# Attention scores from float32 tiles or from three float16 products of cast and added halves

## Chip, core and metric

The kernel runs on one core of a Trainium2 chip. The metric is device time in microseconds of one execution, median of several runs. TensorE (PE) multiplies, VectorE (DVE) and ScalarE (ACT) work on elements, GpSimd (POOL) does some of both, and SP (SyncE) issues transfers. Each engine works through its own instructions in order and waits at an instruction until what it needs is there.

## What is computed

Inputs are q, k, v of 8 batches, 8 heads, 576 positions and 64 values per head. Attention is local: each head's sequence is cut into 9 chunks of 64, and each chunk attends to itself alone.

```python
scores = scale * np.matmul(q_c, k_c.transpose(0, 1, 2, 4, 3))
scores = scores - np.max(scores, axis=-1, keepdims=True)
attn = np.exp(scores)
attn = attn / (np.sum(attn, axis=-1, keepdims=True) + 1e-09)
out = np.matmul(attn, v_c)
```

The result x (8 x 576 x 512) goes through two feed-forward layers: `x + relu(norm(x) @ w_ch1) @ w_ch2`, and then a gated layer with a product over positions and `w_out`. Everything is float32 outside; the kernel writes most products as three float16 products of a high and a low half (high·high, high·low, low·high).

## The kernel before

Attention runs in 36 units t = 0 to 35, each of 128 rows (two chunks side by side) and 8 heads; two units make a block b = t // 2 of the first feed-forward layer. The input `qkv` holds q, k and v of a unit as 128 rows of 1536 float32, q and k next to each other with the head dimension along the partitions.

The order of all work is written by a planner, `Plan`. Each `op(engine, ns, fn, rd, wr, prio, lat)` is an operation with its cost, what it reads and writes, and the latency until other engines see its result. The planner plays a clock: of the operations that are ready on an engine it places the one with the lowest `prio`. The engine then executes in that order, whatever real durations are.

From block 3 on, blocks and attention are merged. For each block, eight steps `ff1p` (L750, first product into two PSUM banks in turn, 24 matmuls, later read by ScalarE at L765) and `ff2p` (L802, second product, two steps behind). Between them L772 to L774 form sums on VectorE, L777 on ScalarE makes the high half and L778 on VectorE the low half. After the steps of block b, the attention units of block b + 2 are emitted (`block(b + 2)`), and the planner mixes them in. The tile names `arena`, `acc` and `bank` belong to this part.

One unit t >= 10 (`JOIN`) goes through these operations:

- `scores(t)`: SP loads q and k (512 KB) into `qkl`, one buffer (L283). `qk` multiplies 16 pairs of 64x64 float32 tiles into `pair` (L291), in four quadrants of the array; the profile shows two records for each float32 multiplication.
- `attention(t)`: maximum (L389), subtraction into `pml` (L390), exponential on ScalarE (L393); `vl` is loaded on SP (L319).
- From t = 14 (`BYDMA`) on, `pml` is split into float16 halves `ph` (L400 on ScalarE, L401 on VectorE), SP transposes them by a transfer into `ptt` (L404), v is split into `vq` (L408, L409), and `pv_` makes 48 float16 products (L349). Units t = 10 to 13 transpose on TensorE into a float32 tile `pt` and multiply in float32 (L361).
- `pv_` of t and `qk` of t + 1 are one planned operation on TensorE (L429): it waits for `ptt`, `vq` and the q and k of the next unit.
- `norm(t)`: statistics (L462, L463), `rs` on GpSimd (L457, L460), `xn` (L466), halves `hl` (L469 on ScalarE, L471 on GpSimd, two buffers), and a transposing transfer on SP into `xT` (L267), which has two buffers and so waits until the first products of block b - 2 are through.

At a block's end L825 and L830 read the sums out of PSUM, L835 on GpSimd adds them, and SP stores them to `x2d` (L677).

Of the kernel before, what the change touches and what calls it, by code (L numbers as in the profile page):

```python
# [9 lines left out]
F16 = mybir.dt.float16  # L10
F32 = mybir.dt.float32
# [3 lines left out]
AF = mybir.ActivationFunctionType  # L15
ALU = mybir.AluOpType
# [8 lines left out]
    a=[2264, -1991, -1698, -26, -1734, 4025, 2562, -374],  # L25
# [4 lines left out]
    lo=[1, 0, 0, 0, 0, 1, 1, 1],  # L30
# [8 lines left out]
    xn=[0, 1, 0, 0, 1, 1, 1, 1],  # L39
    g=[150, 12000, 200, 400, 150],  # L40
    f=[-277, -1680, 2543],
# [9 lines left out]
JOIN = 10  # L51
# [96 lines left out]
def fused_kernel(ctx: ExitStack, tc, qkv, w1, w2, g1, w_in, w_out, wsgt, wsgs, g2, b_sg, out):  # L148
    nc = tc.nc
    PSUM = bass.MemoryType.PSUM  # L150
    P = 128
# [20 lines left out]
    pools = {}  # L172
# [42 lines left out]
    plan = Plan(TUNE['g'][1])  # L215
# [55 lines left out]
    def palloc(tag, bufs, shape, dt, pool=None):  # L271
        return plan.buf(tag, bufs, lambda: (pool or pools["att"][1]).tile(shape, dt, tag=tag, name=tag, bufs=bufs))
# [3 lines left out]
    started = {}  # L276
    BYDMA = 14

    def scores(t, o):

        a = palloc("qk", 2, [P, 2, 512], F32) if t < JOIN else palloc("qkl", 1, [P, 2, 512], F32)
        src = qkv[t].rearrange("p (a f) -> p a f", a=3)
        o("SP", 1700, lambda: nc.sync.dma_start(out=a.t, in_=src[:, 0:2]), wr=[a], lat=2200 if t < JOIN else 4000)  # L283
        s2 = pair[t % 2 if t < 6 else 1]

        def qk():
            for hp in range(4):
                for r in (slice(0, 64), slice(64, 128)):
                    for c in range(2):
                        k = hp * 128 + c * 64  # L290
                        nc.tensor.matmul(  # L291
                            s2[64 * c:64 * c + 64, r.start // 64, hp * 64:hp * 64 + 64],
                            lhsT=a.t[r, 0, k:k + 64],
                            rhs=a.t[r, 1, k:k + 64],
                            start=True,
                            stop=True,
                        )

        started[t] = a, qk

    def attention(t):
        n = t % 2 if t < 6 else 1
        s2, ks = pair[n], f"pair{n}"
        kp = ks if t < JOIN else "pairv"
        pr = TUNE['a'][t] if t < 8 else 10 * t
        lat = TUNE['g'][2] if t < 8 else 300 if t < JOIN else 600 if t < JOIN + 2 else 1000 if t < BYDMA else 400
        far = dict(lat=1500 if t < JOIN + 2 else 3000 if t < BYDMA else 1000) if t >= JOIN else {}
        z = 1

        def o(eng, ns, fn, **k):  # L310
            ns = FAST.get((eng, ns), ns)
            op(eng, ns, fn, prio=k.pop("prio", pr), lat=k.pop("lat", lat), **k)

        if t not in started:
            scores(t, o)
            a, qk = started[t]
            o("PE", 1260 * z, qk, rd=[a], wr=[ks])
        v = palloc("v", 2, [P, 512], F32) if t < JOIN else palloc("vl", 1, [P, 512], F32)
        o("SP", 730, lambda: nc.sync.dma_start(out=v.t, in_=qkv[t].rearrange("p (a f) -> p a f", a=3)[:, 2]), wr=[v], lat=2200)  # L319
        mx = palloc("mx", 2, [P, 2, 4, 1], F32)  # L320
        pm = palloc("pm", 2, [P, 4, 2, 64], F32) if t < JOIN else palloc("pml", 1, [P, 4, 2, 64], F32)
        sm = palloc("sm", 2, [P, 4, 2, 1], F32)
        rd = palloc("rd", 2, [P, 4, 2, 1], F32)
        pt = palloc("pt", 1, [P, 4, 128], F32) if t < BYDMA else None
        if t in (4, 5):
            x = plan.buf(f"x{t}", 1, lambda: pools["att"][1].tile([P, 512], F32, name=f"x{t}", bufs=1))
        else:
            x = palloc("x", 6, [P, 512], F32, px)
# [3 lines left out]
        ptt, vq = [None], [None]  # L332
        pp = lambda: [pt, v] if t < BYDMA else [ptt[0], vq[0]]
# [7 lines left out]
        def pv_():  # L341
            if t >= BYDMA:
                for hp in range(4):
                    for n, (y, z) in enumerate(((0, 0), (0, 1), (1, 0))):
                        for r in (slice(0, 64), slice(64, 128)):
                            for c in range(2):
                                k = c * 256 + hp * 64
                                q = hp * 128 + c * 64
                                nc.tensor.matmul(  # L349
                                    s2[64 * c:64 * c + 64, r.start // 64, 256 + hp * 64:256 + hp * 64 + 64],  # L350
                                    lhsT=ptt[0].t[r, y, q:q + 64],
                                    rhs=vq[0].t[r, z, k:k + 64],
                                    start=(n == 0),
                                    stop=(n == 2),
                                )
                return
            for hp in range(4):
                for r in (slice(0, 64), slice(64, 128)):
                    for c in range(2):
                        k = c * 256 + hp * 64  # L360
                        nc.tensor.matmul(  # L361
                            s2[64 * c:64 * c + 64, r.start // 64, 256 + hp * 64:256 + hp * 64 + 64],
                            lhsT=pt.t[r, hp, 64 * c:64 * c + 64],
                            rhs=v.t[r, k:k + 64],
                            start=True,
                            stop=True,
                        )
# [12 lines left out]
        def sums():  # L380
# [10 lines left out]
            out=pm.t.rearrange("p h a k -> p a h k"), in0=sv, in1=mx.t.to_broadcast([P, 2, 4, 64]), op=ALU.subtract  # L391
# [4 lines left out]
        else:  # L396
            ph = palloc("ph", 1, [P, 2, 512], F16)
# [4 lines left out]
                out=ph.t[:, 1], in0=flat(), in1=ph.t[:, 0], op=ALU.subtract  # L402
            ), rd=[pm], wr=[ph], two=1)
            o("SP", 1100, lambda: nc.sync.dma_start_transpose(  # L404
                out=ptt[0].t.rearrange("p x (h q) -> p (x h) q", h=4), in_=ph.t.rearrange("p x f -> p (x f)")
# [4 lines left out]
                out=vq[0].t[:, 1], in0=v.t, in1=vq[0].t[:, 0], op=ALU.subtract  # L410
# [4 lines left out]
        if t < BYDMA:  # L415
            o("ACT", 480, lambda: nc.scalar.activation(
                out=pt.t.rearrange("p (a h) q -> p a h q", a=2),
                in_=s2[:, :, 0:256].rearrange("p a (h q) -> p a h q", h=2),
                func=AF.Copy,
# [4 lines left out]
        if t < JOIN or t + 1 == NT:  # L424
            o("PE", 1260 * z, pv_, rd=pp(), wr=[kp])
        else:
            scores(t + 1, o)
            a_, qk_ = started[t + 1]
            o("PE", 1260, lambda: (pv_(), qk_()), rd=pp() + [a_], wr=[kp, ks])  # L429
        o("DVE", 600, lambda: nc.vector.tensor_tensor(  # L430
            out=x.t.rearrange("p (h a d) -> p a h d", h=4, a=2),
            in0=pv,
# [6 lines left out]
    def norm(t, x, o):  # L439

        bs = palloc("bs", 2, [P, 6], F32)
        mv = palloc("mv", 2, [P, 2], F32)
        rs = palloc("rs", 2, [P, 1], F32)
        xn = palloc("xn", 1, [P, 512], F32)
        hl = palloc("hl", 2, [P, 2, 512], F16)
        b = t // 2
        c0 = (t % 2 if b < B0 else 1 - t % 2) * 128
        if t % 2 == 0:
            if b == 2:
                xT_t[b] = plan.buf("xT2", 1, lambda: stage.tile([P, 2, 4, 256], F16, name="xT2"))  # L450
            else:
                xT_t[b] = palloc("xT", 2, [P, 2, 4, 256], F16, px)
        xT = xT_t[b]
        x_t[t] = x

        def rs_():
            nc.gpsimd.tensor_scalar(  # L457
                out=rs.t, in0=mv.t[:, 1:2], scalar1=1.0, scalar2=1e-6, op0=ALU.mult, op1=ALU.add
            )
            nc.gpsimd.tensor_tensor(out=rs.t, in0=rs.t, in1=cpow, op=ALU.pow)  # L460

        o("DVE", 600, lambda: nc.vector.bn_stats(out=bs.t, in_=x.t), rd=[x], wr=[bs])  # L462
        o("DVE", 70, lambda: nc.vector.bn_aggr(out=mv.t, in_=bs.t), rd=[bs], wr=[mv])  # L463
        o("POOL", 730, rs_, rd=[mv, "cpow"], wr=[rs], two=2)
        xe = ("POOL", 830, nc.gpsimd) if t < 8 and TUNE['xn'][t] else ("DVE", 460, nc.vector)
        o(xe[0], xe[1], lambda: xe[2].tensor_scalar(  # L466
            out=xn.t, in0=x.t, scalar1=mv.t[:, 0:1], scalar2=rs.t, op0=ALU.subtract, op1=ALU.mult
        ), rd=[x, mv, rs], wr=[xn], two=1 + (xe[0] == "POOL"))
        o("ACT", 520, lambda: nc.scalar.activation(out=hl.t[:, 0], in_=xn.t, func=AF.Copy), rd=[xn], wr=[hl])  # L469
        lo = ("DVE", 600, nc.vector) if t < 8 and TUNE['lo'][t] else ("POOL", 1110, nc.gpsimd)  # L470
        o(lo[0], lo[1], lambda: lo[2].tensor_tensor(  # L471
            out=hl.t[:, 1], in0=xn.t, in1=hl.t[:, 0], op=ALU.subtract
        ), rd=[xn], wr=[hl], two=1)
        o("SP", 1100, lambda: transpose(xT.t, slice(c0, c0 + 128), hl.t), rd=[hl], wr=[xT], lat=2200)
# [379 lines left out]

    bW = {"top": Buf("topB", None)}

    ATT = [f"{n}{k}" for n in ("qk", "v", "mx", "pm", "sm", "rd", "bs", "mv", "rs", "hl") for k in range(2)] + ["pt", "xn", "qkl", "vl", "u0", "u1", "pml", "ph", "ptt", "vq"]
    w2s = {}

    def open_sums():  # L860
# [232 lines left out]
    with tc.manual_schedule():  # L1093
# [127 lines left out]
        vl = fixed("vl", 1, [P, GT, D], F16)  # L1221
# [461 lines left out]
```

## Time and profile before

| | us |
|---|---|
| median of three runs | 1177.54 |
| lowest and highest | 1176.41 and 1178.52 |
| the profiled execution, its own time | 1177.76 |
| its span, first to last instruction | 1175.7 |
| TensorE busy | 1163.7 |
| VectorE busy | 915.2 |
| ScalarE busy | 586.3 |
| GpSimd busy | 196.5 |

The profile's times count from the first instruction of the span. A matmul record is listed with its start and a modelled length, so small matmuls overlap in the list; the distance between starts is the pace. A timeline row merges neighbours: length is from the first start to the last end, and x48 is the number of records. "Landing" of a transfer is the time from issue to its data being there.

### The profile page before, as it was taken

How to read it: one execution, taken by the hardware profiler on the slowest of the kernel's cores; microseconds unless marked ns; L12 is line 12 of the kernel's file. 1: busy time of each engine (PE TensorE's matmuls, PEld its weight loads, DVE VectorE, ACT ScalarE, POOL GpSimd, SP SyncE). 2: the span in 40 equal slices, each digit the busy share in tenths (PEclk: the TensorE clock that was granted, in tenths of full speed). 3: DMA queues.
4: the chain of work that ended last, by engine and by line, in shares of the span. 5: the costliest groups of instructions: out<-in, count | busy, mean ns of one | idle time of the engine just before them, and what ended most of it. 6: DMA issues, size and time to landing. Idle time of an engine off the chain costs nothing.

```text
span 1175.7 us, 27945 instructions
## 1 busy us (share of the span) xinstructions
PE 1163.7 (99%) x11810; PEld 884.4 (75%) x11810; DVE 915.2 (78%) x1744; ACT 586.3 (50%) x854; POOL 196.5 (17%) x279
## 2 busy tenths in 40 slices
PE   8899999999999999999999999999999999999998
PEld 6687448888888888888888888888565566557454
DVE  6997797898898888768877865677889589577555
ACT  5787634665665644434444443345646445434330
POOL 2211010323113112211311322012102001102100
PEclk7999999999999999999999999999999999999999
DMA  8974016544242343244133111436175573372303
GB/s 286 281 242 118 18 28 225 185 111 91 75 93 69 68 100 91 65 82 91 55 89 75 56 46 33 88 86 179 38 140 158 113 149 110 91 123 73 90 1 117
DMA packets 165053, 124.36 MB, mean 106 GB/s; under 512 B 128704, under 2 KB 137792, under 8 KB 164928
## 3 DMA queue, kind: packets, MB, share of 16 engines
q1 hardware_dynamic: 164928, 122.58, 40.2%
q8 instruction: 92, 1.51, 0.5%
q14 instruction: 33, 0.27, 0.1%
HBM read 72.74 MB, written 18.88 MB: 78 GB/s over the span
## 4 chain that ended last, share of the span: by engine, by line
PE 92%; DVE 4%; DMA 2%; ACT 1%; issue 1%; POOL 0%; SPq 0%; ACTq 0%; DVEq 0%
PE bank L750 26%; PE acc L802 23%; PE pb L1478 5%; PE acc L1562 4%; PE pair L659 4%; PE pb L1562 4%; PE acc L1478 3%; PE pb L1382 3%; PE bank L638 3%; PE acc L1424 3%; PE pb L1424 3%; PE acc L1382 3%; PE bank L659 2%; PE pair L291 1%; PE pair L349 1%; PE pb L1479 1%
## 5 line engine op out<-in xcount | busy, mean ns | idle before, releaser
L750 PE MATMUL bank<-xT,w1h 128*128 128x256 f16 x1920 | 321.0, 273 | 0.0
L802 PEld LDWEIGHTS <-arena 128*128 128x128 f16 x2520 | 244.5, 98 | 29.7 <-DVE arena L778 0.2
L750 PE MATMUL bank<-xT,w1l 128*128 128x256 f16 x960 | 261.7, 273 | 0.0
L802 PE MATMUL acc<-w,arena 128*128 128x256 f16 x1440 | 218.3, 273 | 0.0
L750 PEld LDWEIGHTS <-w1h 128*128 128x128 f16 x1920 | 187.7, 98 | 22.1
L777 ACT ACTIVATE arena<-arena 128x896 f16<-128x896 f32 x120 | 113.9, 949 | 159.3 <-DVE arena L774 75.4
L802 PE MATMUL acc<-w2s,arena 128*128 128x256 f16 x1080 | 177.2, 273 | 0.0
L778 DVE TENSOR_TENSOR arena<-arena 128x896 f16<-128x896 f32 x120 | 130.3, 1086 | 39.5 <-ACT arena L777 39.1
L765 ACT ACTIVATE arena<-bank 128x512 f32<-128x512 f32 x120 | 71.4, 595 | 121.2 <-PE bank L750 120.6
L835 POOL TENSOR_TENSOR x<-x,u 128x256 f32<-128x256 f32 (+1 forms) x65 | 62.6, 989 | 259.2 <-DVE x L825 157.7
L750 PEld LDWEIGHTS <-w1l 128*128 128x128 f16 x960 | 93.9, 98 | 10.8
L772 DVE TENSOR_TENSOR arena<-arena 128x256 f32<-128x256 f32 x120 | 57.2, 477 | 37.1 <-ACT arena L765 36.1
L1562 PEld LDWEIGHTS <-w2s 128*128 128x128 f16 x444 | 43.4, 98 | 47.3
L1382 PEld LDWEIGHTS <-x2T 128*128 128x128 f16 x672 | 65.6, 98 | 9.8
L638 PE MATMUL bank<-xT,w1h 128*128 128x256 f16 x384 | 64.4, 273 | 1.1 <-DMA xT<-hl 0.7
L773 DVE TENSOR_TENSOR arena<-arena 128x256 f32<-128x256 f32 x120 | 59.1, 492 | 4.1
L1424 PEld LDWEIGHTS <-late 128*128 128x128 f16 x336 | 32.7, 98 | 39.2
L471 POOL TENSOR_TENSOR hl<-xn,hl 128x512 f16<-128x512 f32 x32 | 43.1, 1346 | 72.9 <-ACT hl L469 68.6
L1478 PEld LDWEIGHTS <-vh 128*128 128x128 f16 x288 | 28.6, 99 | 33.2
L1562 PE MATMUL acc<-wout,w2s 128*128 128x512 f16 (+1 forms) x252 | 53.3, 369 | 0.0
L638 PE MATMUL bank<-xT,w1l 128*128 128x256 f16 x192 | 52.3, 273 | 0.0
L1478 PE MATMUL pb<-wsg,vh 128*128 128x512 f16 x166 | 51.6, 380 | 0.0
(287 smaller groups left out, 2050.7 us busy)
## 6 DMA issues: line engine op xcount, KB each, us to landing
straw<-in_w SPq DMA_DIRECT2D x16, 1023.8 KB, 6.2
qkl<-in_qkv SPq DMA_DIRECT2D x26, 512.0 KB, 3.9
x2d<-x SPq DMA_DIRECT2D x36, 256.0 KB, 2.0
xs<-x2d SPq DMA_DIRECT2D x27, 256.0 KB, 4.2
vl<-in_qkv SPq DMA_DIRECT2D x26, 256.0 KB, 3.2
w2s<-x2d SPq DMA_DIRECT2D x21, 256.0 KB, 2.8
out<-w2s SPq DMA_DIRECT2D x21, 256.0 KB, 3.1
qk<-in_qkv SPq DMA_DIRECT2D x10, 512.0 KB, 4.8
```

The costliest lines, as they stand in the source:

```text
L638: nc.tensor.matmul(acc, lhsT=w[j][:, k, fc], rhs=xT.t[:, x, k], start=(n == 0), stop=(n == 11))
L659: nc.tensor.matmul(acc[i], lhsT=h[x].t[:, c], rhs=w2t[j][:, f % 2, y], start=(f == 0 and n == 0), stop=(f == NF - 1 and n == 2),)
L750: nc.tensor.matmul(acc[:, y * 256:y * 256 + 256], lhsT=w[j][:, k, fc], rhs=xT.t[:, x, k], start=(n == 0), stop=(n == 11),)
L765: op("ACT", 500, lambda: nc.scalar.activation(out=o.t[:, 0:4].rearrange("p n t -> p (n t)"), in_=acc, func=AF.Relu, scale=0.5), rd=[kb] + ...
L777: op("ACT", 860, lambda: nc.scalar.activation(out=h.t[:, 0], in_=o.t[:, 1:8], func=AF.Copy), rd=[o] + ar, wr=[h], prio=-100)
L778: op("DVE", 1010, lambda: nc.vector.tensor_tensor(out=h.t[:, 1], in0=o.t[:, 1:8], in1=h.t[:, 0], op=ALU.subtract), rd=[o, h], wr=[h.key + ...
L802: nc.tensor.matmul(acc, lhsT=h.t[:, x, n], rhs=r(y), start=(first and j == 0 and m == 0), stop=(j == 7 and m == 2), skip_group_check=True,)
L835: op("POOL", ns, lambda: nc.gpsimd.tensor_tensor(out=d(), in0=d(), in1=v(), op=ALU.add), rd=u + ["q6", "q5", "q7"], wr=[x], prio=-50, two=1)
L1382: nc.tensor.matmul(ap[:, q * 256:q * 256 + 256], lhsT=xT[:, x, a, k, c], rhs=right(b, 1, k, w), start=(first and n == 0), stop=(k == 1 and ...
L1424: nc.tensor.matmul(ap, lhsT=right(b, 0, k, w)[:, m * 128:m * 128 + 128], rhs=xT[:, x, a, k], start=(first and n == 0), stop=(k == 1 and w ...
L1478: nc.tensor.matmul(ap, lhsT=v[:, fc], rhs=w[:, 0:512], start=(n == 0), stop=end)
L1562: nc.tensor.matmul(ap[:, 0:m], lhsT=x[:, k, c], rhs=w[:, k, fc], start=(n == 0), stop=(n == 11))
```

## The change

From t = 10 on, q and k are no longer loaded as float32. A transfer issued by GpSimd casts them to float16 on the way into `qh`; ScalarE writes the negative of `qh` into `ql`; a second transfer from GpSimd reads q and k again and adds them to `ql`, which then holds the low half. `qh` and `ql` have two buffers each. The scores are three float16 products (48 matmuls in place of 16 float32 ones). The latencies handed to the planner are 7000, 3000 and 8000 ns. To make room, `hl` has one buffer from t = 10 on (`hll`), and `pt` of t = 10 to 13 lies in the buffer of `ptt`. The product of the two low halves is left out, as in the kernel's other split products.

```diff
     def scores(t, o):
-        a = palloc("qk", 2, [P, 2, 512], F32) if t < JOIN else palloc("qkl", 1, [P, 2, 512], F32)
         src = qkv[t].rearrange("p (a f) -> p a f", a=3)
-        o("SP", 1700, lambda: nc.sync.dma_start(out=a.t, in_=src[:, 0:2]), wr=[a], lat=2200 if t < JOIN else 4000)
         s2 = pair[t % 2 if t < 6 else 1]
+        if t >= JOIN:
+            hi, lo = (palloc(n, 2, [P, 2, 512], F16) for n in ("qh", "ql"))
+            o("POOL", 700, lambda: nc.gpsimd.dma_start(out=hi.t, in_=src[:, 0:2]), wr=[hi], lat=7000)
+            o("ACT", 1050, lambda: nc.scalar.activation(out=lo.t, in_=hi.t, func=AF.Copy, scale=-1.0), rd=[hi], wr=[lo], lat=3000)
+            o("POOL", 920, lambda: nc.gpsimd.dma_start(
+                out=lo.t, in_=src[:, 0:2], accum_op=ALU.add
+            ), wr=[lo], lat=8000)
+
+            def qk():
+                for hp in range(4):
+                    for n, (y, z) in enumerate(((hi, hi), (hi, lo), (lo, hi))):
+                        for r in (slice(0, 64), slice(64, 128)):
+                            for c in range(2):
+                                k = hp * 128 + c * 64
+                                nc.tensor.matmul(
+                                    s2[64 * c:64 * c + 64, r.start // 64, hp * 64:hp * 64 + 64],
+                                    lhsT=y.t[r, 0, k:k + 64],
+                                    rhs=z.t[r, 1, k:k + 64],
+                                    start=(n == 0),
+                                    stop=(n == 2),
+                                )
+
+            started[t] = [hi, lo], qk
+            return
+        a = palloc("qk", 2, [P, 2, 512], F32)
+        o("SP", 1700, lambda: nc.sync.dma_start(out=a.t, in_=src[:, 0:2]), wr=[a], lat=2200)
...
-        pt = palloc("pt", 1, [P, 4, 128], F32) if t < BYDMA else None
+        pt = None
+        if t < JOIN:
+            pt = palloc("pt", 1, [P, 4, 128], F32)
+        elif t < BYDMA:
+            pt = plan.buf("ptt", 1, lambda: pools["att"][1].tile(
+                [P, 2, 512], F16, tag="ptt", name="ptt", bufs=1
+            ).rearrange("p x f -> p (x f)").bitcast(F32).rearrange("p (h q) -> p h q", h=4))
...
-            o("PE", 1260, lambda: (pv_(), qk_()), rd=pp() + [a_], wr=[kp, ks])
+            o("PE", 1260, lambda: (pv_(), qk_()), rd=pp() + a_, wr=[kp, ks])
...
-        hl = palloc("hl", 2, [P, 2, 512], F16)
+        hl = palloc("hl", 2, [P, 2, 512], F16) if t < JOIN else palloc("hll", 1, [P, 2, 512], F16)
```

## Rows read from the trace of the kernel before

**Rows 1.** The page: busy us (share of the span) and instructions of each engine.

```profile
PE 1163.7 (99%) x11810; PEld 884.4 (75%) x11810; DVE 915.2 (78%) x1744; ACT 586.3 (50%) x854; POOL 196.5 (17%) x279
```

**Rows 2.** Windows: start:end, length, busy us of each engine, PEclk, DMA share, GB/s.

```profile
180.00:430.00 250.00, 249.40 (x3150) 221.57 (x3148) 219.44 (x427) 149.89 (x214) 53.57 (x61) 1.00 0.44 116
430.00:700.00 270.00, 270.00 (x3354) 240.18 (x3352) 209.60 (x399) 114.28 (x167) 59.17 (x73) 1.00 0.31 73
```

**Rows 3.** One line's view of L404: the transposes into `ptt`.

```profile
L404 SPq DMA_TRANSPOSE ptt<-ph x22: 1231/1249/4409, 255.7 to 678.0; - x22
...
DMA to landing us min/median/max: 3.0/3.2/6.2
```

**Rows 4.** Timeline of TensorE: start us, length us, instruction, records, [idle before].

```profile
425.64 0.58 PE L349 MATMUL pair<-vq,ptt 64*64 64x64 f16 x48 [0.60 <-DMA ptt<-ph]
...
488.64 0.57 PE L349 MATMUL pair<-vq,ptt 64*64 64x64 f16 x48
...
502.78 0.49 PE L802 MATMUL acc<-w,arena 128*128 128x256 f16 x3
...
503.76 0.49 PE L802 MATMUL acc<-w2s,arena 128*128 128x256 f16 x3
504.19 0.58 PE L349 MATMUL pair<-vq,ptt 64*64 64x64 f16 x48
504.59 0.70 PE L291 MATMUL pair<-qkl 64*64 64x64 f32 x32
505.21 0.83 PE L802 MATMUL acc<-w,arena 128*128 128x256 f16 x6
...
530.21 0.57 PE L349 MATMUL pair<-vq,ptt 64*64 64x64 f16 x48
```

**Rows 5.** Timeline of TensorE at the last unit.

```profile
696.47 0.57 PE L349 MATMUL pair<-vq,ptt 64*64 64x64 f16 x48
696.97 0.50 PE L802 MATMUL acc<-w,arena 128*128 128x256 f16 x3
```

**Rows 6.** The tile `qkl`: durations min/median/max in ns, first and last start.

```profile
L291 PE MATMUL pair<-qkl x832: 218/218/267, 187.8 to 671.3; 64*64 64x64 f32 x167
L283 SPq DMA_DIRECT2D qkl<-in_qkv x26: 328/333/1619, 180.7 to 656.0; - x26
...
DMA to landing us min/median/max: 3.3/3.9/12.0
```

**Rows 7.** Timeline of TensorE at the scores of t = 11.

```profile
198.69 0.65 PE L291 MATMUL pair<-qkl 64*64 64x64 f32 x32
199.27 0.50 PE L802 MATMUL acc<-w,arena 128*128 128x256 f16 x3
```

**Rows 8.** Groups of ScalarE by form: busy us, mean ns, idle before.

```profile
L984 ACT ACTIVATE late<-tmp 128x1024 f16<-128x1024 f32 x8 | 8.4, 1048 | 0.1
```

**Rows 9.** Timelines of ScalarE and VectorE in a steady unit.

```profile
498.07 0.60 ACT L765 ACTIVATE arena<-bank 128x512 f32<-128x512 f32 x1
...
497.02 1.08 DVE L778 TENSOR_TENSOR arena<-arena 128x896 f16<-128x896 f32 x1
498.02 0.53 DVE L466 TENSOR_SCALAR xn<-x,mv,rs 128x512 f32<-128x512 f32 x1
```

**Rows 10.** One line's view of L835 on GpSimd.

```profile
L835 POOL TENSOR_TENSOR x<-x,u x65: 723/733/1541, 230.8 to 732.0; 128x256 f32<-128x256 f32 x52, 128x512 f32<-128x512 f32 x13
```

**Rows 11.** Timelines of TensorE (first line) and SP at the first units.

```profile
178.58 0.38 PE L750 MATMUL bank<-xT,w1h 128*128 128x256 f16 x2
...
180.72 0.33 SPq L283 DMA_DIRECT2D qkl<-in_qkv  x1
...
220.88 1.24 SPq L267 DMA_TRANSPOSE xT<-hl  x1
```

**Rows 12.** Waits of SP's queue: waited for, us in total, times, longest.

```profile
SPq L283 <- PE pair L291: 75.7, 21, 4.8
```

**Rows 13.** Timeline of SP in a steady unit.

```profile
499.19 1.24 SPq L404 DMA_TRANSPOSE ptt<-ph  x1
```

More of the change, by code (lines that the diff above doesn't have):

```diff
@@ L297, in qk @@
                         )
-        started[t] = a, qk
+        started[t] = [a], qk
     def attention(t):
@@ L316, in attention @@
             a, qk = started[t]
-            o("PE", 1260 * z, qk, rd=[a], wr=[ks])
+            o("PE", 1260 * z, qk, rd=a, wr=[ks])
         v = palloc("v", 2, [P, 512], F32) if t < JOIN else palloc("vl", 1, [P, 512], F32)
@@ L855, in fused_kernel @@
     bW = {"top": Buf("topB", None)}
-    ATT = [f"{n}{k}" for n in ("qk", "v", "mx", "pm", "sm", "rd", "bs", "mv", "rs", "hl") for k in range(2)] + ["pt", "xn", "qkl", "vl", "u0", "u1", "pml", "ph", "ptt", "vq"]
+    ATT = [f"{n}{k}" for n in ("qk", "v", "mx", "pm", "sm", "rd", "bs", "mv", "rs", "hl") for k in range(2)] + ["pt", "xn", "qh0", "qh1", "ql0", "ql1", "hll", "vl", "u0", "u1", "pml", "ph", "ptt", "vq"]
     w2s = {}
```

## Prediction

> **What bounds the kernel now.** I read the page's totals first: TensorE is busy for 99% of the span, VectorE 78%, ScalarE 50%, GpSimd 17% [rows 1]. Then, by windows, the stretch that the change touches: the attention units from the eleventh on (t = 10 to 35) run between 187 [rows 6] and 697 us [rows 5], inside the merged block loop. There TensorE is idle 0.60 us of 520, at a granted clock of 1.00 [rows 2], so only two things move the end: fewer TensorE microseconds, or a new wait on TensorE. The one wait that is there, 0.60 us before 425.64, is for `ptt` [rows 4]; I leave it as it is.
>
> **TensorE.** A late unit is one planned operation, `pv_` and then `qk_` of the next unit. In a steady one the block products before run in steps of 0.109 (nine from 502.78 to 503.76 [rows 4]), so the last three are through at 504.09; the 48 float16 products of L349 start at 504.19, the 32 records of L291 at 504.59, the next block product at 505.21. So 48 float16 records take 0.40 us when other small tiles follow, and 32 float32 records 0.62 with the way back to 128-wide tiles. What is that way back worth? The last unit has `pv_` alone: 0.50 us from 696.47 to 696.97 [rows 5], so 0.10. The new score burst, 48 float16 records in the form of L349, should take 0.40 + 0.10 = 0.50. Saving: 0.62 − 0.50 = 0.12 us per unit. There are 832 / 32 = 26 units [rows 6]: 26 × 0.12 = 3.1 us.
>
> Bounds of it. Below: behind a float32 `pv_` (t = 11 to 13) L291 took 0.58 [rows 7], and 0.58 − 0.50 = 0.08 gives 2.1 us. Above: if the way back costs nothing behind float16 scores, 0.62 − 0.40 = 0.22 gives 5.7 us. Another lower end: 96 records in one burst were never run; if each goes at the rate of the float32 ones (0.62 / 32 = 0.0194), the burst takes 0.93 and the change costs 26 × 0.31 = 8.1 us. I take 0.12, since L349 is the same form, tile and type.
>
> The rows put the float16 rate at three products for 0.40 where float32 took 0.62 − 0.10 = 0.52. The Trainium skill, FP8 and Floating Point Precision, § TensorE Precision Notes, counts true float32 as four passes; three in place of four would save a quarter of 0.52, 0.13 per unit and 3.4 us in all (an estimate from that page). The trace is close to it and a little under.
>
> **ScalarE.** 26 new passes over 128x1024 float16. The nearest row, L984 writing the same shape from float32, is 1.05 us [rows 8]: 27 us more on an engine that is busy 264 of 520 us in the stretch [rows 2]. It costs nothing while the evacuations L765 and L777 stay in time. The cover is measurable: the halves of one step are finished by L778 at 498.10 [rows 9], and the block product that reads them starts at 502.78 [rows 4]: 4.7 us of slack. One pass of 1.05 fits in it; without cover each would cost up to its own 1.05.
>
> **GpSimd.** Per unit two transfer issues. The trace has none on this engine; bounds are the 0.33 us that SP takes for L283 [rows 6] and the longest form of L835, 1.54 [rows 10]. I take 1.0, between the planner's 700 and 920 and the upper row: 52 us more, on an engine busy 113 of 520 [rows 2]. Its order is that of the planner and it waits in order: the adding transfer waits for the ScalarE pass, and behind it stand `rs` (L457, L460), the low half of `hl` (L471) and the adds of L835. Who waits for those? The `xT` transposes, which feed a block loop one 41.6 us period later; and L835's sums go out to `x2d`, read at the end. A few microseconds there reach nothing.
>
> **The chain of the halves.** By the planner: issue 0.7, landing 7.0, pass 1.05, gap 3.0, issue 0.9, landing 8.0, together 20.7 us. Two buffers each mean that unit t+1's first transfer may start once `qk` of t−1 is done. Starts of L349 in the steady stretch are 488.64, 504.19 and 530.21 [rows 4]: 41.6 us from the first to the third, 20 more than the chain. With `qk` done at 489.66 (488.64 + 1.02) and a gap of 0.4, the pass is planned for 497.8. Shorter gaps stand only at the start: unit t = 10 now loads at 180.72 [rows 11] and multiplies at 187.8 [rows 6]; the longer chain puts it near 201, some 14 us later. TensorE has block products to fill with, and the `xT` of that pair is needed two loops after the first one begins, at about 178.6 + 2 x 41.6 = 262, while its second transpose now goes out at 220.88 [rows 11]: 14 us later is still early.
>
> **SP.** 26 issues of L283 leave SP's queue, with the places where SP stands waiting for a `qk` before it: 75.7 us in total [rows 12]. Queued behind were `vl`, `ptt` and `xT`. None of these was late on TensorE but once, so I count zero gain here.
>
> **Single `hl` and `pt` in `ptt`.** The next unit's `hl` now waits until the transpose of the one before has landed. Both `xT` transposes of a pair wait for the end of a block loop anyway; the second moves later by a landing (3.2 us for `ptt`, the same kind [rows 3]), a ScalarE and a GpSimd pass, some 5 us in all, against a need one loop of 41.6 us on. `pt` shares its buffer with `ptt` in four units and had one buffer before: nothing.
>
> **Transfers.** 512 KB per unit go out of SP's queue, twice 512 KB are read on the new one. Engines of the DMA were busy 31 to 44% of the stretch [rows 2]. What may collide is `ptt`: in every second of its 22 units [rows 3] (issued at 499.19 [rows 13], used at 504.19) it has 5.0 us from issue to use and lands in 3.2, slack 1.8. By the chain above the cast runs at 490 to 498 and the adding transfer starts at about 502, when `ptt` has landed. I count zero; each microsecond beyond the slack would cost 11 us.
>
> **Sum.** The profiled execution took 1177.76 us, a span of 1175.70 and 2.06 around it. 1177.76 − 3.1 = 1174.6; the median of the three runs is 0.2 below that execution, so **1174.4**.
>
> **Rivals.**
> *Late halves, slower.* The place is ScalarE's queue: the pass waits for the cast transfer, planned 7.0 us after issue, and L765 of the next bank stands behind it (498.07 [rows 9], just after the planned 497.8). The slack of 4.7 makes 11.7 us the deciding point; beyond it each microsecond is lost 26 times. For it: `qkl`, the same bytes uncast, once took 12.0. Against it: its median is 3.9 [rows 6], and even 3.3 more for a doubled path stays under 8. At 13 us: 26 × 1.3 − 3 = +31, about 1208. Chance 0.10.
> This rival has a page: the Trainium skill, SBUF — State Buffer, § Who interferes with whom, says that a transfer issued from GpSimd starves of descriptors while VectorE runs a two-port instruction, and advises the hardware queues. The nearest candidate here, L466, takes 0.53 us per unit [rows 9], far less than the 4.7 of slack; the trace of before holds no such transfer, so it shows neither.
> *Slow burst.* 96 small products in a row cannot be fed at 0.40 per 48: +8.1 us, 1185.6. Against it, 48 and 32 in a row were. Chance 0.10.
> *Given back.* TensorE saves its 3 us, but a reordered plan brings new waits for `ptt` or `xT` of 1 to 4 us in total: TensorE takes the order of the planner and stands still where a load is late, as with 0.60 before 425.64 [rows 4]; five such waits are the whole gain. About 1177. Chance 0.27.
> *All hidden, the forecast.* 0.53, own range 1171.8 to 1175.4 by the two savings.
>
> **Numbers.** A measurement here tells about 0.2%, 2.4 us, from no change. The forecast's gain of 3.1 lies just beyond it; of its 0.53 I give 0.44 to faster and 0.09 to same. Given back: 0.02 faster, 0.17 same, 0.08 slower. The other two are slower, 0.20. Faster 0.46, same 0.26, slower 0.28. The range goes from the upper saving with the 0.60 us wait gone as well (1171) to the slow burst (1186); it leaves out the late halves and what lies past its ends, together under 0.2.
>
> **What would show it.** Right: L291's place shows 48 float16 records for each of 26 units, and `pv` to next block product takes 0.90 us instead of 1.02; idle TensorE in 180 to 700 stays under 1 us; ScalarE's new pass is 1.05 and its idle time before L765 stays "PE bank". Wrong: idle time before L349, the score products, L750 or L802 put down to `ql`, `ptt` or the ScalarE chain; a new transfer that lands later than 8 us; or a burst that takes over 1.1.

## The result, and the profile after

The changed kernel takes 1184.96 us (median of 6 runs, 1181.96 to 1186.09) against 1178.17 for the kernel before on the same chip (6 runs, 1176.41 to 1179.33): a ratio of 1.0058, 95% interval 1.0047 to 1.0069. It is slower by 6.8 us. The forecast was 1174.4 and faster.

TensorE first, by the same windows as [rows 2], columns the same:

```profile
180.00:430.00 250.00, 245.36 (x3252) 217.84 (x3251) 214.44 (x422) 158.54 (x223) 73.81 (x90) 1.00 0.62 116
430.00:700.00 270.00, 267.43 (x3571) 237.63 (x3570) 201.19 (x392) 125.31 (x180) 74.39 (x94) 1.00 0.43 73
```

TensorE now stands idle for 4.64 + 2.57 = 7.21 us of the stretch, where it was 0.60. The granted clock is 1.00 as before, and the share of busy DMA engines went from 0.44 and 0.31 to 0.62 and 0.43. The view of waits says for what TensorE stands still (180 to 800 us; total us, times, longest):

```profile
PE pair L379 <- DMA ptt<-ph: 5.5, 8, 1.9
PE pair L379 <- DVE x L460: 1.3, 1, 1.3
```

L379 is `pv_`, and 5.5 of the 7.2 us are waits for `ptt`, the transpose of the softmax numerators. Its landing time, to be held against [rows 3]:

```profile
L434 SPq DMA_TRANSPOSE ptt<-ph x22: 1232/1248/2351, 281.2 to 684.2; - x22
...
DMA to landing us min/median/max: 3.0/3.7/8.8
```

The chain that ended last passes through eight such transposes. Here is one in a steady unit (start, length):

```profile
504.52 1.19 PE acc L832 x11
505.71 5.14 DMA ptt<-ph
510.85 0.04 issue
510.89 0.58 PE pair L379 x48
```

In the unit of [rows 13] this transpose had landed unnoticed. The timeline shows what runs beside it now:

```profile
503.94 0.63 ACT L430 ACTIVATE ph<-pml 128x512 f16<-128x512 f32 x1
504.47 1.04 ACT L286 ACTIVATE ql<-qh 128x1024 f16<-128x1024 f16 x1
505.71 1.24 SPq L434 DMA_TRANSPOSE ptt<-ph  x1
505.94 0.90 POOL L287 DMA_DIRECT2D ql<-in_qkv  x1 [2.62 <-ACT ql L286]
510.89 0.58 PE L379 MATMUL pair<-vq,ptt 64*64 64x64 f16 x48 [0.15 <-DMA ptt<-ph]
511.29 0.21 PE L297 MATMUL pair<-qh 64*64 64x64 f16 x4
511.83 0.83 PE L832 MATMUL acc<-w,arena 128*128 128x256 f16 x6
```

The adding transfer goes out 0.23 us after `ptt`. The same pairing recurs at 463.72/463.95, 547.31/547.54, 589.71/589.94 and 631.43/631.67; in these five units `ptt` takes 5.1 to 5.9 us, and TensorE waits 0.15 to 0.96 us, 2.2 us in all. The other three waits, 3.3 us, are earlier, where the adding transfer goes out just before `ptt` (at 280.35, 299.16 and 423.31). From the chain:

```profile
281.24 5.38 DMA ptt<-ph
299.24 8.84 DMA ptt<-ph
424.70 6.04 DMA ptt<-ph
```

The last three lines of the timeline also give the new burst: 511.83 − 511.29 = 0.54 us for the scores where float32 took 0.62, and 0.94 from `pv` to the next block product where it was 1.02 [rows 4].

To keep the first 180 us apart, in which all kernels here run the same instructions in the same order, I read the first and last start of the first block products, ff1p (first line: before; second: after):

```profile
L750 PE MATMUL bank<-xT,w1h x1920: 272/273/283, 178.6 to 793.5; 128*128 128x256 f16 x192
L780 PE MATMUL bank<-xT,w1h x1920: 270/273/284, 180.9 to 801.1; 128*128 128x256 f16 x192
```

This stretch is 620.2 us long; before it was 614.9. So 5.3 us are lost inside it; the rest of the span behind it is 382.0 against 382.2. By the terms: 6.6 us more idle, 26 × 0.08 = 2.1 us less for scores, together +4.5. The other 0.8 no row shows.

### The profile page after: what moved, and what is told of

Same layout as the page of the kernel before. It is cut to its first block, busy times and chain, and to the rows that moved or that the text cites. A ratio compares the mean times of both kernels' runs of the same rounds, so it can differ in the third digit from the quotient of the medians.

```text
span 1183.1 us, 28869 instructions
## 1 busy us (share of the span) xinstructions
PE 1163.2 (98%) x12226; PEld 884.0 (75%) x12226; DVE 907.5 (77%) x1744; ACT 607.9 (51%) x880; POOL 233.8 (20%) x331
## 3 DMA queue, kind: packets, MB, share of 16 engines
q0 software_dynamic: 7488, 13.63, 10.1%
## 4 chain that ended last, share of the span: by engine, by line
PE 88%; DMA 7%; DVE 3%; ACT 1%; issue 1%; POOL 0%; SPq 0%; ACTq 0%
PE bank L780 23%; PE acc L832 20%; PE pb L1508 5%; PE acc L1592 4%; DMA ptt<-ph 4%; PE pair L689 4%; PE pb L1592 4%; PE bank L668 3%; PE acc L1508 3%; PE pb L1412 3%; PE acc L1454 3%; PE pb L1454 3%; PE acc L1412 3%; PE bank L689 2%; PE pair L379 1%
## 5 line engine op out<-in xcount | busy, mean ns | idle before, releaser
L795 ACT ACTIVATE arena<-bank 128x512 f32<-128x512 f32 x120 | 70.9, 591 | 96.4 <-PE bank L780 95.6
L802 DVE TENSOR_TENSOR arena<-arena 128x256 f32<-128x256 f32 x120 | 55.7, 464 | 39.0 <-ACT arena L795 38.7
L1359 POOL TENSOR_SCALAR rs<-mv 128x2 f32<-128x2 f32 (+1 forms) x20 | 6.4, 319 | 260.4 <-DVE mv L1354 257.5
L501 POOL TENSOR_TENSOR hll<-xn,hll 128x512 f16<-128x512 f32 x26 | 34.9, 1344 | 115.8 <-ACT hll L499 108.7
L803 DVE TENSOR_TENSOR arena<-arena 128x256 f32<-128x256 f32 x120 | 53.6, 447 | 4.1
```

What stands on the lines that cost most here:

```text
L795: op("ACT", 500, lambda: nc.scalar.activation(out=o.t[:, 0:4].rearrange("p n t -> p (n t)"), in_=acc, func=AF.Relu, scale=0.5), rd=[kb] + ...
```

## The experiments

The question was whether the adding transfer, by running beside the tight `ptt` (the one with some 5 us from issue to use), causes the stall. Rivals were the memory (single `hll`, shared `ptt` buffer), the cast transfer, the order of the engines, the float16 burst, and a later start of the program. All times below are medians; each ratio is to runs of before on the same chip as that run. The last three columns come from one profiled execution each: "stretch" is the ff1p stretch; "idle" is TensorE's in 180 to 700 us; "ptt" is the median and longest landing.

| run | time us | ratio to before, 95% | stretch | idle | ptt |
|---|---|---|---|---|---|
| before | 1178.17 | | 614.9 | 0.60 | 3.2 / 6.2 |
| after | 1184.96 | 1.0047 to 1.0069 | 620.2 | 7.21 | 3.7 / 8.8 |
| e1 no adding transfer | 1176.67 | 0.9975 to 0.9994 | 612.4 | 0.46 | 3.2 / 4.6 |
| e2 plain cast in its place | 1184.15 | 1.0037 to 1.0061 | 621.8 | 8.96 | 3.6 / 6.7 |
| e3 adding only after `ptt` | 1178.32 | 0.9996 to 1.0021 | 612.4 | 0.47 | 3.1 / 4.5 |
| e4 halves made on engines | 1189.98 | 1.0090 to 1.0123 | 628.6 | 11.03 | 3.3 / 5.0 |
| e5 before, memory changes only | 1176.32 | 0.9976 to 0.9997 | 614.2 | 0.00 | 3.1 / 8.2 |
| e6 no software transfers | 1177.73 | 0.9980 to 0.9999 | 612.3 | 0.19 | 3.1 / 4.7 |
| e7 pass and adding 5 us later | 1182.28 | 1.0019 to 1.0037 | 615.9 | 3.03 | 3.1 / 7.3 |
| e8 adding twice | 1230.23 | 1.0428 to 1.0455 | 668.2 | 41.85 | 5.4 / 7.5 |
| e9 a sixteenth of the bytes | 1176.43 | 0.9977 to 1.0000 | 613.3 | 1.01 | 3.5 / 4.7 |
| e10 as e3, even units only | 1178.13 | 0.9990 to 1.0016 | 619.0 | 4.72 | 3.1 / 4.8 |
| e11 after, second profile | 1181.99 | one run | 619.1 | 5.93 | 3.5 / 8.0 |
| e12 one `ql`, two `hll` | 1185.31 | 1.0046 to 1.0073 | 623.8 | 8.52 | 4.0 / 8.3 |

**e1, the suspect taken away.**

```diff
-            o("POOL", 920, lambda: nc.gpsimd.dma_start(
-                out=lo.t, in_=src[:, 0:2], accum_op=ALU.add
-            ), wr=[lo], lat=8000)
+            o("POOL", 920, lambda: nc.gpsimd.memset(lo.t[:, 1, 511:512], 0.0), wr=[lo], lat=8000)
```

> The adding transfer is replaced by a memset of one column on the same queue, at the same place in the planner's order; the low half then stays the negated high half, so that part of the computation is left out. Theory (the adding transfer shares the DMA engines with the ptt transpose that is issued at the same moment, the transpose lands in 5.1 to 6.0 us instead of 3.2, and TensorE waits): ptt lands in 3.2 to 3.7 everywhere, idle TensorE between 180 and 700 us falls from 7.2 us to about 1, time about 1185 - 6 = 1179 us. Rival memory (the single hll and the shared ptt buffer): nothing changes, 1185. Rival cast (the cast transfer, not the adding one, delays ptt or xT): 1185. Rival burst: 1185.

Its windows:

```profile
180.00:430.00 250.00, 249.54 (x3383) 221.89 (x3382) 218.60 (x428) 161.05 (x226) 64.88 (x91) 1.00 0.45 102
430.00:700.00 270.00, 270.00 (x3557) 240.43 (x3555) 205.13 (x399) 125.65 (x181) 67.20 (x95) 1.00 0.30 63
```

What is left of TensorE's waits, 180 to 800 us:

```profile
PE pair L377 <- DVE x L458: 0.5, 1, 0.5
```

The idle time goes from 7.21 to 0.46 us and no wait for `ptt` is left, while memory, cast, ScalarE pass and products stay. The stretch is 7.8 us shorter.

**e3, all work kept, only the moment changed.** GpSimd reads one column of `ptt` of unit t−2 ahead of the adding transfer of unit t.

```diff
+            o("POOL", 100, lambda: nc.gpsimd.tensor_copy(out=seen, in_=ptt[0].t[:, 0, 0:1]), rd=[ptt[0]], wr=[f"seen{t}", "seen"])
...
-            ), wr=[lo], lat=8000)
+            ), rd=[f"seen{t - 2}"] if t >= BYDMA + 2 else [], wr=[lo], lat=8000)
```

> Before each adding transfer GpSimd reads one column of the ptt of two units earlier, so the transfer is issued only once that transpose has landed; all work is kept. Theory: ptt lands in about 3.2 to 3.7 us in the tight units too, the idle TensorE between 180 and 700 us falls from 7.2 to about 1, time 1178 to 1179 us, and below 1178 if the first 180 us come out as in the kernel before. Rivals memory, cast, burst: 1185. If the added wait on GpSimd holds up the norm: over 1185.

One steady unit of its timeline:

```profile
540.16 1.28 SPq L435 DMA_TRANSPOSE ptt<-ph  x1
543.26 0.66 POOL L438 COPY seen<-ptt 128x1 f16<-128x1 f16 x1 [5.49 <-DMA ptt<-ph]
543.88 0.92 POOL L288 DMA_DIRECT2D ql<-in_qkv  x1
...
545.12 0.58 PE L380 MATMUL pair<-vq,ptt 64*64 64x64 f16 x48
```

Left alone, `ptt` lands in 3.1 us, and `pv` starts 4.96 us after the issue of `ptt` without a wait. The same bytes on the same queue cost nothing 3.7 us later. The stretch is 612.4, as in e1; the time came out level with before rather than below, with runs from 1175.21 to 1182.82 (see e10).

**e2, is it the addition?**

```diff
-                out=lo.t, in_=src[:, 0:2], accum_op=ALU.add
+                out=lo.t, in_=src[:, 0:2]
```

> The second transfer writes a plain float16 cast instead of adding (accum_op left out), at the same place and with the same bytes read; the low half then is a second copy of the high half, so that part of the computation is changed. Theory: the transfer's own engine time decides; a cast without the addition holds the engines less long (the cast lands in 4.3 us, the adding one in 6.3), so ptt in the tight units lands between 3.2 and 5.4, idle TensorE between 180 and 700 us falls from 7.2 to 2 to 5, time 1179 to 1183. If the addition alone is the cause: ptt 3.2, about 1177 as without the transfer. If any software transfer of that size at that moment costs the same: 1184 to 1185.

Its view of TensorE's waits, 180 to 800 us:

```profile
PE pair L379 <- DMA ptt<-ph: 6.9, 6, 1.7
```

No: a plain cast in that place stalls TensorE as much (`ptt` takes 6.0 to 6.7 us in the same five units), and the time is that of the changed kernel. My theory's 1179 to 1183 was too low; what counts is a transfer of this size there. That it has to be a software one is not shown: in the kernel before, the longest landing of `ptt`, 6.2 us, came beside `qkl` and `vl` on SP's own queue.

**e9, bytes or presence?**

```diff
-                out=lo.t, in_=src[:, 0:2], accum_op=ALU.add
+                out=lo.t[:, 0, 0:64], in_=src[:, 0, 0:64], accum_op=ALU.add
```

> The adding transfer keeps its place, its queue, its add and its 128 rows, but moves only 64 of the 1024 columns, a sixteenth of the bytes; the rest of the low half stays the negated high half. Theory, by bytes: ptt in the tight units lands in 3.2 to 3.5 us, the ff1p stretch is about 612.5 us, time 1175 to 1178. Rival, by the mere presence of a software transfer (its descriptors or its issue on GpSimd) beside the transpose: ptt 5 us, the stretch 620, time 1184 to 1185.

Its view of the tile `ptt`:

```profile
DMA to landing us min/median/max: 3.0/3.5/4.7
```

The same queue, add and 128 rows with a sixteenth of the bytes: `ptt` takes 3.5 to 3.8 us in the five units and never more than 4.7, and TensorE does not wait for it. The software queue's packets are as many as in the kernel after (7488 in both profiles). So neither the presence of the transfer nor its number of packets does it; the bytes decide.

**e8, the transfer issued twice.** The adding transfer is issued by a loop `for _ in range(2)`.

> The adding transfer is issued twice in a row at its place; the low half is then wrong by one more copy, the rest stays. Theory: ptt in the tight units lands later by about as much again as one adding transfer cost (3.2 with none, 5.1 to 6.0 with one, so 6 to 8 us), and since the 1.8 us of slack are gone already, each microsecond more is paid in 8 to 11 units: the ff1p stretch grows by 8 to 25 us, time 1193 to 1210. Rivals memory and burst, and a cause in the order of the engines alone: 1185 to 1187.

Its windows, its view of the tile `ptt`, and GpSimd in a steady unit:

```profile
180.00:430.00 250.00, 225.24 (x2906) 196.73 (x2905) 188.29 (x371) 146.32 (x208) 71.89 (x90) 0.96 0.65 116
430.00:700.00 270.00, 252.91 (x3327) 223.29 (x3327) 189.58 (x376) 118.10 (x170) 82.73 (x105) 0.99 0.58 87
```

```profile
DMA to landing us min/median/max: 3.0/5.4/7.5
```

```profile
498.90 0.93 POOL L289 DMA_DIRECT2D ql<-in_qkv  x1 [2.59 <-ACT ql L286]
505.42 0.87 POOL L289 DMA_DIRECT2D ql<-in_qkv  x1 [5.59 <-DMA ql<-in_qkv]
```

The time is 45 us over after, where at most 25 were expected, and the mechanism was not the one in the theory. GpSimd waits until the first transfer has landed before it issues the second, so the two never run side by side. In the tight units `ptt` takes 5.3 to 5.7 us, no more than with one transfer, where 6 to 8 were expected. This run is therefore no test of more bytes beside one transpose. What it adds are GpSimd's waits for its own transfers, 137 us in all; behind them stand the low half of `hll` and the adds of L867, and TensorE now also waits for `arena`, `u` and `x` from VectorE. The transposes of the other units meet software transfers too, hence the median of 5.4.

Part of the loss is the clock, 0.96 and 0.99 in the windows. In five stretches, 23.8 us together, the granted clock is about 0.50, the lower of the two levels (1.2 GHz). Each begins while TensorE stands idle for 2.4 to 5.6 us, or just after; one of them, and the product that ends the idle time:

```profile
295.50:302.30 6.80, 4.80 (x23) 3.35 (x24) 6.47 (x14) 2.49 (x3) 4.49 (x6) 0.50 0.66 140
```

```profile
297.50 0.39 PE L834 MATMUL acc<-w,arena 128*128 128x256 f16 x1 [4.84 <-DVE arena L810]
```

Half of 23.8 is some 12 of the 48 us by which the stretch is longer than after's. In after both windows give 1.00.

**e5 and e6, what the rest of the change is worth.** e5 is the kernel before with `hll` and the shared `ptt` buffer; e6 is after with both transfers replaced by memsets.

```diff
-        hl = palloc("hl", 2, [P, 2, 512], F16)
+        hl = palloc("hl", 2, [P, 2, 512], F16) if t < JOIN else palloc("hll", 1, [P, 2, 512], F16)
```

```diff
-            o("POOL", 700, lambda: nc.gpsimd.dma_start(out=hi.t, in_=src[:, 0:2]), wr=[hi], lat=7000)
+            o("POOL", 700, lambda: nc.gpsimd.memset(hi.t, 0.0), wr=[hi], lat=7000)
```

> The kernel before with only the two changes of memory: one hll from the eleventh unit on, and pt in ptt's place. Theory: 1178 us, idle TensorE between 180 and 700 us still about 0.6. Rival memory: 1183 to 1185 us, with TensorE waiting for hll's transpose or ptt.

> Both software transfers are replaced by memsets of the halves' buffers on GpSimd; nothing of queries and keys is loaded from the eleventh unit on, so the scores are left out in value but every product, the ScalarE pass and the buffers stay. Theory: only the TensorE saving is left: the stretch from the first to the last ff1p product is 612 to 613 us as in the run without the adding transfer (614.2 in the kernel before with the changed buffers), time 1175 to 1177. If the cast transfer too had cost something on the path: below 611 us and 1175. If the programs with a software queue start later (their first ff1p product came at 179.8 to 180.9, that of the others at 177.5 to 178.9): the first ff1p product at 177.5 to 179 here.

Memory is not the cause: e5 has no idle TensorE at all in the stretch. Between the two the stretch falls from 614.2 to 612.3, and without e6's 0.2 of idle by 2.1 us. That is the whole gain of the float16 products, 26 × 0.08. Since e1 keeps the cast and has the same stretch as e6, the cast costs nothing.

**e7, the same repair by the order.** `lat=7000` of the cast becomes `lat=12000`.

> All work kept; the planner is told that the cast takes 12.0 us to land instead of 7.0, so it puts the ScalarE pass, and with it the adding transfer, about 5 us later in the order. Theory: where the adding transfer now starts after ptt has landed, ptt takes 3.2 us and the stall goes: the ff1p stretch 612 to 614 us, time 1176 to 1179. If the new order puts it beside the next ptt or the transpose of hll in some units: 1180 to 1185. Rival ScalarE (the pass itself, not the transfer, is in the way): no change, 1185.

The two longest of its waits of TensorE:

```profile
PE pair L379 <- DVE x L460: 1.6, 2, 1.1
PE acc L832 <- DVE arena L808: 0.7, 2, 0.4
```

In the units with a tight `ptt` the adding transfer now follows it by 6.5 us or more (502.70/509.17, 584.87/591.59), and no wait for `ptt` is left. The new order brings small waits for VectorE instead, 3.0 us of idle in all, and the stretch is 615.9. Of the stretch's loss 4.3 of 5.3 us come back; of the medians' distance to before 3.5 of 6.8 (1182.28 against 1178.96 on its chip). The time is over the 1176 to 1179 that was expected.

**e4, no software transfer at all.**

```diff
+            a = palloc("qkl", 1, [P, 2, 512], F32)
+            o("SP", 1700, lambda: nc.sync.dma_start(out=a.t, in_=src[:, 0:2]), wr=[a], lat=4000)
+            hi, lo = (palloc(n, 1, [P, 2, 512], F16) for n in ("qh", "ql"))
+            o("ACT", 1050, lambda: nc.scalar.activation(out=hi.t, in_=a.t, func=AF.Copy), rd=[a], wr=[hi], lat=3000)
+            o("POOL", 2300, lambda: nc.gpsimd.tensor_tensor(out=lo.t, in0=a.t, in1=hi.t, op=ALU.subtract), rd=[a, hi], wr=[lo], two=1)
```

> The halves are made on the engines: the sync queue loads float32 as before, ScalarE casts (1.05 us), GpSimd subtracts (about 2.3 us); no software transfers, the float16 products and the shared buffers stay. Theory: the stall on ptt is gone and the TensorE saving of 26 x 0.08 = 2.1 us is left: about 1176 us, ptt lands in 3.2. Rival memory: about 1183 or more, since the shared buffers stay. Rival burst (the float16 products themselves cost): 1183 or more. If GpSimd's 26 x 2.3 us collide with VectorE or the low half of hll: ptt or xT late by it, over 1180.

A miss: 1189.98 where about 1176 was expected. `qkl`, `qh` and `ql` have one buffer each here. The timeline shows a new collision:

```profile
281.03 2.13 POOL L288 TENSOR_TENSOR ql<-qkl,qh 128x1024 f16<-128x1024 f32 x1
281.07 2.37 DVE L801 TENSOR_TENSOR arena<-arena 128x256 f32<-128x256 f32 x1
...
283.48 0.42 DVE L802 TENSOR_TENSOR arena<-arena 128x256 f32<-128x256 f32 x1
```

L801 takes 0.42 us in the median and 2.37 beside GpSimd's subtraction. The Trainium skill, SBUF — State Buffer, § Who interferes with whom, says that a VectorE instruction with two SBUF inputs contends with a GpSimd one that reads SBUF, over a port pair that is an exclusive lock; this trace agrees: L801 ends 0.28 us after the subtraction. How much of the 13 us between e4 and e1 this collision makes was not tried. Of TensorE's 11.0 us of idle 6.3 are waits for VectorE (`arena` and `u`) and 2.6 for `ptt`; and in two stretches of 3.4 us, behind waits of 2.65 and 2.87 us, the granted clock is about 0.50, some 3.4 us more.

**e10 to e12, the scatter, and a better version.** e10 is e3 with the wait in even units only (`t % 2 == 0` on both lines), e11 the changed kernel again.

> As the version that waits for ptt, but only in the even units, whose ptt is the tight one (10 waits instead of 20); all work kept. Theory: only the tight transposes cost, so the ff1p stretch is again 612 to 613 us, time 1175 to 1178. If the odd units' transposes matter too: 614 to 617 us, time up to 1181.

> The changed kernel once more, for a second profile. Theory: the stretch from the first to the last ff1p product repeats (620.2 us before, within 1 us), with 6 to 8 us of idle TensorE put down to ptt, while the first ff1p product, which lies behind work that no kernel here changes, falls anywhere between 177 and 181 us. Rival start (the changed program begins later): it falls at 180.5 to 181.5 again.

e10's median is level with before, but its runs range from 1176.37 to 1184.34, and the profiled one is the longest: its stretch is 619.0 where 612 to 613 was expected. Its chain near 390 us:

```profile
386.33 9.73 DMA xT<-hll
...
396.15 0.13 ACT hll L502
```

This transpose of `hll` was issued between an adding transfer (384.88) and a cast (387.72) and took 9.73 us. With one `hll`, ScalarE's next `hll` pass stood behind it, and TensorE stood idle for 3.1 us until 405; behind that the granted clock is 0.51 for 3.4 us, another 1.7 us lost. So the single buffer, free in e5, can be felt once software transfers run beside `xT`. That e3's longer runs are of this kind is possible but was not shown. e11 repeats the stretch (619.1), with 4.5 us of waits for `ptt` where 6 to 8 were expected.

```diff
-            hi, lo = (palloc(n, 2, [P, 2, 512], F16) for n in ("qh", "ql"))
+            hi, lo = (palloc(n, k, [P, 2, 512], F16) for n, k in (("qh", 2), ("ql", 1)))
...
-        hl = palloc("hl", 2, [P, 2, 512], F16) if t < JOIN else palloc("hll", 1, [P, 2, 512], F16)
+        hl = palloc("hl", 2, [P, 2, 512], F16) if t < JOIN else palloc("hll", 2, [P, 2, 512], F16)
```

> The changed kernel with one ql buffer instead of two and the 2 KB that this frees given back to hll, which has two again; all work kept. With one ql, ScalarE's pass and the adding transfer of unit t+2 can start only after the products of unit t+1, which follow pv of unit t and so its ptt: the order alone keeps the adding transfer off the tight ptt, and a late transpose of hll no longer holds ScalarE. Theory: ptt in the tight units 3.0 to 3.7 us, the ff1p stretch 612 to 613 us, time 1174.5 to 1177, and runs that lie closer together than those of the two versions that wait for ptt (1175.2 to 1182.8 and 1176.4 to 1184.3). If ScalarE's pass, queued behind the products, holds the evacuations behind it: the stretch over 616, time over 1180.

A miss: after 430 us TensorE has no idle time at all, but in the early units the order changed and one `xT` comes 6 us late, and around it the granted clock is 0.50 for 6.8 us, 3.4 us lost; the time is 1185.31. The first line of its waits of TensorE:

```profile
PE bank L780 <- DMA xT<-hll: 6.0, 1, 6.0
```

**The start.** The first ff1p product came at 177.3 to 181.2 us over all runs. Without a software queue (before, e4, e5, e6) it came at 178.6, 177.5, 178.9 and 179.4; with one at 180.9 and 178.8 (the two profiles of after) and at 180.6, 177.9, 179.8, 180.2, 177.3, 178.0, 181.2 and 178.4 (e1, e2, e3, e7, e8, e9, e10, e12). The means are 178.6 and 179.3, and the two groups overlap: the 2.3 us between the first two profiles are mostly scatter, and a later start of some 0.7 us is neither shown nor excluded. Medians differ by 6.8 and the stretches by 4.2 to 5.3 us, so some 2 us of the difference stay unplaced.

No version here keeps all work and beats both kernels by more than the 0.2% that can be told; the nearest is e5, 1.5 us under before on its chip, which has no float16 scores.

## Why the prediction was wrong, point by point

**The chain of the halves and Transfers: the step that failed.** The prediction placed the adding transfer "at about 502, when `ptt` has landed". Relative to the cast issue (496.62 in the profile after) the ScalarE pass came 7.85 us later, as planned, and `ptt` 9.09 later, where the prediction had 499.19 [rows 13] against a start at 490. But the 3.0 us between pass and adding transfer are only an allowance in the planner: GpSimd was idle and issued the transfer 0.43 us after the pass had ended (505.51 to 505.94). That moved it from `ptt`'s end to its start. In the three early units it went out even before `ptt`. The second half of the step, zero for a collision, was never priced: side by side, `ptt` needs 5.1 to 5.9 us, where 5.0 were there. "Each microsecond beyond the slack" was the right form: in the five steady units `ptt` lands 0.2 to 1.0 us beyond it, and TensorE waits 0.15 to 0.96. Why the one transfer lengthens the other the runs do not show by themselves. The Trainium skill, DMA: Bandwidth & Descriptors, § SWDGE vs HWDGE vs iDMA, says that software and hardware queues feed different queues inside each DMA engine, which takes them in turn. By that rule more bytes on the one would lengthen the other; e1 and e9 agree, and e8 does not bear on it.

**Given back** was the rival that came about, with 7.2 us of waits where it allowed 1 to 4. That 1184.96 lies inside the stated range of 1171 to 1186 is luck: its upper end stood for the slow burst, which did not come.

**TensorE**: right in kind, mis-sized. 0.12 us per unit was forecast and 0.08 measured (the lower bound given), 2.1 us in place of 3.1. The burst took 0.54 instead of 0.50. *Slow burst* is refuted.

**ScalarE and Late halves**: right. The new pass takes 1.04 us, the evacuation L795 still waits for "PE bank" (70.6 of 71.3 us between 180 and 700), and ScalarE waited 0.4 us in all for a cast, which landed within 9.1 us at the longest, under the deciding 11.7. One sign of being wrong, a new transfer landing later than 8 us, did come (9.1 and 11.3 us), but TensorE never waited for `qh` or `ql` in that profile.

**SP**: zero gain, as said. Between e5 and e6, where L283 has left SP's queue, the stretch falls by the products' 2.1 us alone.

**GpSimd**: 0.58 and 0.90 us per issue against 1.0 each, hidden as said. The transfers landed in 4.3 and 6.3 us (medians); the tiles `qh` and `ql` of the kernel after:

```profile
L285 POOL DMA_DIRECT2D qh<-in_qkv x26: 542/578/787, 183.4 to 638.1; - x26
...
DMA to landing us min/median/max: 3.6/4.3/9.1
```

```profile
L287 POOL DMA_DIRECT2D ql<-in_qkv x26: 847/898/948, 194.0 to 647.6; - x26
...
DMA to landing us min/median/max: 5.1/6.3/11.3
```

**Single `hl` and `pt` in `ptt`**: nothing, as said, by e5; with software transfers beside `xT` not quite nothing, by e10. The scores of t = 10 came at 207.15, not near 201, and that cost nothing.

## What to carry to other kernels

When a change adds a transfer, list the transfers already in flight at the moment it is released, and compare their slack with a landing stretched by the newcomer's bytes; a mean DMA share of 0.4 says nothing on that. A latency written in a planner orders the work but delays nothing: here the freed engine issued 0.43 us after what it waited for, not 3.0. Where a tight transfer can't be moved, tie the newcomer to its landing, and then look at the next transfer that it meets.

## What was not expected of the hardware

A software transfer that reads 512 KB stretched an SBUF transpose of 256 KB, issued 0.2 us before it, from 3.1 to 5.1–5.9 us; a plain cast stretched it to 6.0–6.7, and a sixteenth of the bytes left it at 3.5–3.8. A GpSimd subtraction of 2.13 us held a VectorE instruction of 0.42 us (median) for 2.37.
